# Batch 0's local q and k turned in halves, and batch 1's strided q and k loaded and turned earlier, in a fused sparse attention and MLP kernel

## The chip, the cores and the metric

The kernel runs on one core of a Trainium2 chip. The core has a tensor engine (PE, with its weight loads shown apart as PEld), a vector engine (DVE), a scalar engine (ACT), GpSimd (POOL) and a sync engine (SP) that only issues transfers. Each engine works through its own queue in order, and waits on semaphores where an instruction needs another engine's result or a transfer's landing. The metric is the device time of one execution in microseconds (us); lower is better.

## The reference

```python
# attention: batch 8, heads 8, sequence 576, head size 64; stride 32
scores = scale * np.matmul(q, k.transpose(0, 1, 3, 2))
rel = pos[:, None] - pos[None, :]
mask_local = (rel >= 0) & (rel < stride)                                     # heads 0 to 3
mask_strided = (rel >= 0) & (pos[None, :] % stride == pos[:, None] % stride) # heads 4 to 7
attn = softmax(np.where(masks, scores, -1e9)); attn_out = np.matmul(attn, v)
# MLP on x = attn_out as 4608 tokens of 512
h = x @ w_in                                  # 512 to 2048
g = np.maximum(h, 0.0) + alpha * np.minimum(h, 0.0)
out = g @ w_out                               # 2048 to 512
```

Both masks are sparse: a local query sees 32 keys at most, a strided one at most 18, so the kernel computes only blocks that can be nonzero.

## The kernel before

The 4608 tokens are nine chunks of 512. Each chunk goes through layer 1 (16 pieces of 128 hidden units, four matmuls each, `lin1_piece`) and layer 2. The attention of the eight batches is spread between these matmuls, so that TensorE always has some. Attention works on pairs of heads, four pairs a batch: pairs 0 and 1 are batch 0's local heads, 2 and 3 its strided heads, 4 and 5 batch 1's local heads, 6 and 7 its strided heads, and so on. This change touches only the opening, which is written out by hand: everything before layer 1 of chunk 0 (all of batch 0's attention), layer 1 of chunk 0, and a second list that mixes chunk 0's layer 2 with batch 1's attention. After that a planner spreads the pieces of later batches evenly.

The lists are made of short functions, and `keep` holds every engine to the order in which they are written:

- `F(nm, pr)` (`turn_first`) transposes batch 0's strided q or k on PE in float32. `G(nm, pr)` (`turn_second`, lines 160 to 169) does the same for batch 1 from the float16 tiles `qsd` and `ksd`, eight transposes and one copy: ACT copies q, DVE copies k. `pr` is 0 for the first strided pair of a batch, 1 for the second.
- `Cl(b, nm, eng)` (`cast_l`) casts local q or k (the tiles `ql` and `kl`) from float32 to float16 on POOL or ACT. `T(u, nm)` (`transpose_piece`, lines 254 to 273) then transposes it on PE, nine transposes into two PSUM banks of five and four, and copies the two banks out with ACT or DVE.
- `Sc(g, i)` (`score_piece`) computes half i of a pair's scores. Half 0 uses the double bank `sp` and one exponential on ACT; half 1 takes two single banks and two exponentials. `sc1(g)` (`score_both`) does both halves and masks them on DVE.
- `Pv(g, a)` (`pv_piece`) multiplies by V, then DVE takes the reciprocal of the sums (L413) and the product (L415).
- `X(g)` (`x_piece`) transposes a pair's output into the layer input `xT` and copies it out with ACT or DVE.
- `vs(b, pr)` casts strided V, `ov(b, eng, c0, c1)` (`over_v`) copies 32 rows of local V for the blocks c0 to c1, each from where the transfer put them to where the next block needs them.
- `L(m)` runs the first two of the four matmuls of layer 1's piece m; `lin1_piece(0, m)` later adds the other two. Each piece is followed by ACT (`neg`, L593) and DVE (`gT`, L596).
- `U(kf)` and `W(i)` are matmuls of chunk 0's layer 2. `w(1)` is one matmul on zeros, `alpha` a small transpose for the slopes.

PSUM has eight banks: three in the pool `ps`, three in `ph` (tag `hps`, used by layer 1 and by half 1 of the early scores), two in `sp`. The zero matmuls hold one `hps` bank until the last of them. Transfers that cast or that come late are issued from POOL's queue: V, W_in in four quarters, then batch 1's strided q and k (`load_d(1)`), its strided V, W_out in four quarters, batch 1's local q, k and V. POOL has eight transfers under way at most: the ninth waits for the first to land. SP's queue issues batch 0's q and k.

Of the kernel before, what the change touches and what calls it, by code (L numbers as in the profile page):

```python
# [10 lines left out]
F16 = mybir.dt.float16  # L11
# [21 lines left out]
def kernel(  # L33
# [10 lines left out]
    nc = tc.nc  # L44
    keep = tc.keep_in_program_order
# [11 lines left out]
    hpool = ctx.enter_context(tc.tile_pool(name="half", bufs=4))  # L57
# [5 lines left out]
    pspool = ctx.enter_context(tc.tile_pool(name="ps", bufs=3, space=bass.MemoryType.PSUM))  # L63
    phpool = ctx.enter_context(tc.tile_pool(name="ph", bufs=3, space=bass.MemoryType.PSUM))
# [9 lines left out]
    ident = consts[:, 0:128]  # L74
# [10 lines left out]
    qTs = [cpool.tile([128, 2, 672], F16, name=f"qT{i}") for i in range(2)]  # L85
    kTs = [cpool.tile([128, 2, 672], F16, name=f"kT{i}") for i in range(2)]
# [7 lines left out]
    loaded = {}  # L94
    cast16 = {}
# [32 lines left out]
                keep(nc.sync.dma_start_transpose(  # L128
                    o.rearrange("r (w p) -> r w p", p=96), t16[0:96, 768 * e : 768 * e + 768]))

    def load_d(b):

        for nm, src in (("q", q), ("k", k)):
            keep(nc.gpsimd.dma_start(
                qks[nm][0:72], src[b, 4:8, :, :].rearrange("h (p t) d -> p h (t d)", t=8)))

# [40 lines left out]
    def cast_l(b, nm, eng="pool"):  # L177
        t16 = hpool.tile([128, 9, 2, 64], F16, tag=f"{nm}l16", bufs=2, name=f"{nm}l16")
        cast_copy(eng, t16, loaded[(b, False, nm)].rearrange("p f (t d) -> p t f d", t=9))
        cast16[(b, False, nm)] = t16  # L180

    def load_v(b, strided):


        if strided:
            st = spool.tile([128, 2048], F16, tag="v", bufs=2, name="stv")
            step = 2 if b == 0 else 4
            for h in range(0, 4, step):
                keep(nc.gpsimd.dma_start(
                    st[0:72, 512 * h : 512 * (h + step)].rearrange("p (h e) -> p h e", h=step),  # L190
                    v[b, 4 + h : 4 + h + step, :, :].rearrange("h (p t) d -> p h (t d)", t=8)))
            loaded[b] = st
        else:
            v16 = vls[b % 2]
            base = v[b, 0:1, 0:1, :]
            r0 = 32 if b < 2 else 0
            step = 12 if b == 0 else 24
            for c in range(0, 24, step):
                keep(nc.gpsimd.dma_start(
                    v16[r0:128, c : c + step, 0:64],  # L200
                    bass.AP(tensor=base.tensor, offset=base.offset + (96 * c - 32 + r0) * D,
                            ap=[[D, 128 - r0], [96 * D, step], [1, D]])))
            cast16[(b, False, "v")] = v16

    def cast_copy(eng, o, i):
        if eng == "act":
            keep(nc.scalar.copy(o, i))
        elif eng == "dve":
            keep(nc.vector.tensor_copy(o, i))
        else:  # L210
            keep(nc.gpsimd.tensor_copy(o, i))  # L211

    def cast_v(b, pr, eng):

        v16 = vss[b % 2]
        cast_copy(eng, v16[0:72, 2 * pr : 2 * pr + 2, :, 0:64],
                  loaded[b][0:72, 1024 * pr : 1024 * pr + 1024].rearrange(
                      "p (h t d) -> p h t d", h=2, t=8))
        cast16[(b, True, "v")] = v16
# [12 lines left out]
    wide = {"on": True}  # L232
# [232 lines left out]
    def T(u, nm):  # L465
        return lambda: transpose_piece(u, nm)

    def Sc(g, i):
        return lambda: score_piece(pairs[g], i)

    def Pv(g, i):
        return lambda: pv_piece(pairs[g], i)

    def X(g, eng=None):
        return lambda: x_piece(pairs[g], eng or ("act" if pairs[g].strided else "dve"))

    for g in range(7, npair + 2):
        c = g // 4
        a, p, t = g, g - 1, g + 1
# [279 lines left out]
    def warm(n):  # L759

        for _ in range(n):
            keep(nc.tensor.matmul(wps, wrm[:, 0:128], wrm, start=True, stop=True))  # L762
# [11 lines left out]
            name=nc.get_next_instruction_name(), act_func_set_id=6, ins=[], outs=[]  # L774
# [35 lines left out]
    def F(nm, pr):  # L810
        return lambda: turn_first(nm, pr)
# [3 lines left out]
        keep(nc.tensor.transpose(apt[:, 0:16], alpha_r, id32[0:16, 0:16]))  # L815
        keep(nc.vector.tensor_scalar(oma, apt[:, 0:16], -1.0, 1.0, op0=ALU.mult, op1=ALU.add))

    def vs(b, pr):
        return lambda: cast_v(b, pr, "dve")

    def Cl(b, nm, eng="pool"):
        return lambda: cast_l(b, nm, eng)

    def ov(b, eng, c0, c1):
        return lambda: over_v(b, eng, c0, c1)

    def w(n):
        return lambda: warm(n)

    def L(m):  # L830
        return lambda: lin1_piece(0, m, True)

    def G(nm, pr):
        return lambda: turn_second(nm, pr, "act" if nm == "q" else "dve")

    warm(17)
    for fn in [
        F("q", 0), w(1), F("k", 0), w(1), F("k", 1), Sc(2, 0), vs(0, 0), w(1), F("q", 1), Sc(2, 1), alpha, Pv(2, 0),
        Sc(3, 1), vs(0, 1), Cl(0, "q"), Cl(0, "k"), Pv(2, 2), Sc(3, 0), w(1), Pv(3, 2), T(0, "q"), Pv(3, 0), w(1),
        Pv(3, 1), w(1), T(0, "k"), X(3), w(1), Sc(0, 1), Pv(2, 1), Sc(0, 0), Sc(1, 1), ov(0, "dve", 12, 24),  # L840
        ov(0, "pool", 0, 12), Pv(0, 1), X(2), Pv(0, 0), Sc(1, 0), Pv(1, 1), L(1), X(0, "act"), Pv(1, 0), L(2), L(3),
        X(1), L(0)]:
        fn()
    load_d(1)
    load_v(1, True)
    load_w(0, True)
    load_w(1, True)
# [2 lines left out]
    load_w(2, True)  # L850
    load_v(1, False)
    load_w(3, True)
    mid = {13: ("q", 0), 14: ("k", 0), 15: ("q", 1)}
    for m in range(16):
        lin1_piece(0, m)
        attn_n(0, 0)
# [14 lines left out]
    def U(kf):  # L871
        def run():
            if kf == 0:
                banks.extend(phpool.tile([128, 512], F32, tag="hps", name="ops") for _ in range(3))
            for mt in range(3):
                keep(nc.tensor.matmul(  # L876
                    banks[mt], gTs[0][:, kf, 128 * mt : 128 * mt + 128], wout16[:, kf, :],
                    start=(kf == 0), stop=(kf == 15)))
            if kf == 15:
                for mt in range(3):  # L880
                    osb = opool.tile([128, 512], F32, tag="osb", name="osb")
                    cast_copy("dve" if mt == 1 else "act", osb, banks[mt])
                    keep(nc.sync.dma_start(out[128 * mt : 128 * mt + 128, :], osb))
        return run
# [14 lines left out]
    def sc1(g):  # L899
        return lambda: score_both(pairs[g], "dve")  # L900

    for fn in [
        U(0), Cl(1, "q"), G("k", 1), vs(1, 0), vs(1, 1), sc1(6), U(1), U(2), sc1(7), Cl(1, "k", "act"), U(3), U(4), loads2,
        Pv(6, 0), Pv(7, 0), Pv(6, 2), U(5), Pv(7, 1), U(6), T(2, "q"), U(7), Pv(7, 2), T(2, "k"), Pv(6, 1), U(8),
        X(7, "dve"), W(0), W(1), sc1(4), U(9), W(2), sc1(5), W(3), ov(1, "dve", 0, 24), W(4), U(10), X(6), U(11),
        Pv(4, 1), W(5), Pv(4, 0), Cl(2, "q", "act"), U(12), Cl(2, "k", "act"), Pv(5, 1), U(13), U(14), Pv(5, 0), U(15), W(6), X(5), X(4), W(7)]:
        fn()
# [65 lines left out]
```

## Time and profile before

| what | value |
|---|---|
| median of 3 runs | 300.79 us (300.78 to 301.1) |
| profiled execution | 300.67 us, its span 298.9 us, granted clock 1.0 |
| PE busy in the span | 292.9 us (98%) |
| DVE, ACT, POOL busy | 219.1, 178.8, 172.8 us |
| matmuls of layer 1 (L585) | 576, 131.9 us of PE |
| first local scores of batch 0 | 17.41 us from the span's start |
| long run of layer 1 matmuls begins | 22.93 us |

The time of an execution is the span, in which instructions of the program run, and some 1.8 us around it. PE's busy time covers a matmul from its start to its modelled end, and matmuls overlap, so a PE that shows as busy may be waiting for a short while; the distance from one start to the next tells more. Below, a bracket at the end of a row gives the idle time of the engine ahead of it and what ended that.

### The profile page before, as it was taken

The numbers are of one execution on the slowest core, as the hardware profiler recorded it, in microseconds if no ns is written. First come the engines' busy times: TensorE is split into PE (matmuls) and PEld (weight loads), VectorE is DVE, ScalarE is ACT, GpSimd is POOL, SyncE is SP. The second block draws the span as 40 slices with busy tenths as digits, with TensorE's granted clock in tenths as the row PEclk, the third lists the DMA queues.
The fourth block names the chain that finished last, engine by engine and source line by source line (L and its number), as shares of the span: only waits on it lengthen the run. The fifth ranks groups of instructions, "written<-read, shape, count | busy, mean of one in ns | idle before, by whom it ended". The sixth has DMA issues, their size and how long they took to land.

```text
span 298.9 us, 6826 instructions
## 1 busy us (share of the span) xinstructions
PE 292.9 (98%) x2683; PEld 183.0 (61%) x2683; DVE 219.1 (73%) x408; ACT 178.8 (60%) x332; POOL 172.8 (58%) x160
## 2 busy tenths in 40 slices
PE   8999999999999999999999999999999999999995
PEld 3764555554545478646864687468745974784484
DVE  5677886668775897589848984898489958936852
ACT  1676755698457775776477646764676356516730
POOL 8362270049969998979897988495653405002300
PEclk9999999999999999999999999999999999999999
DMA  7999999999998969999989999955911040022004
GB/s 183 257 193 202 256 197 259 217 200 295 113 200 140 113 101 97 159 190 132 127 156 182 158 139 188 170 89 96 205 24 21 16 148 0 2 72 70 0 2 141
DMA packets 96977, 41.18 MB, mean 138 GB/s; under 512 B 75361, under 2 KB 93233, under 8 KB 96945
## 3 DMA queue, kind: packets, MB, share of 16 engines
q0 software_dynamic: 51008, 17.77, 60.7%
q1 hardware_dynamic: 45584, 22.32, 34.6%
q10 hardware_dynamic: 352, 0.66, 0.9%
q8 instruction: 21, 0.34, 0.5%
q14 instruction: 12, 0.09, 0.1%
HBM read 38.24 MB, written 9.44 MB: 160 GB/s over the span
## 4 chain that ended last, share of the span: by engine, by line
PE 82%; DVE 10%; ACT 3%; issue 3%; DVEq 0%; ACTq 0%
PE hps L585 37%; PE ops L720 18%; PE ops L624 5%; PE ops L710 4%; PE pv L406 4%; DVE gsum L654 2%; PE wps L762 2%; PE ops L876 2%; DVE gT L596 2%; DVE x L415 2%; PE sp L353 2%; DVE x16s L415 1%; ACT neg L593 1%; PE sph L353 1%; PE xp L431 1%
## 5 line engine op out<-in xcount | busy, mean ns | idle before, releaser
L585 PE MATMUL hps<-xT,win 128*128 128x512 f16 x576 | 131.9, 379 | 0.0
L596 DVE SCALAR_TENSOR_TENSOR gT<-neg,oma,hps 128x512 f16<-128x512 f32 x144 | 105.3, 744 | 36.1 <-ACT neg L593 28.1
L593 ACT ACTIVATE neg<-hps 128x512 f32<-128x512 f32 x144 | 85.8, 598 | 35.2 <-PE hps L585 33.0
L585 PEld LDWEIGHTS <-win 128*128 128x128 f16 x576 | 53.7, 98 | 58.9 <-issue 0.2
L654 POOL TENSOR_TENSOR gsum<-gT 128x1024 f16<-128x1024 f16 x14 | 29.7, 2123 | 41.7 <-DVE gT L596 36.7
L378 POOL TENSOR_TENSOR et<-et,consts 128x576 f16<-128x576 f16 (+1 forms) x24 | 35.5, 1481 | 30.2 <-ACT et L376 30.0
L720 PEld LDWEIGHTS <-gT 128*128 128x128 f16 x336 | 31.5, 98 | 5.4 <-issue 0.3
L415 DVE TENSOR_TENSOR x<-pv,rc 96x384 f16<-96x384 f32 (+2 forms) x62 | 33.0, 532 | 2.1
L385 POOL TENSOR_TENSOR et<-et,consts 128x576 f16<-128x576 f16 (+1 forms) x24 | 31.5, 1313 | 0.0
L406 PEld LDWEIGHTS <-et 72*128 72x128 f16 (+1 forms) x448 | 23.4, 98 | 11.5 <-issue 1.2
L720 PE MATMUL ops<-wout,gT 128*128 128x256 f16 x224 | 27.9, 272 | 0.1
L710 PE MATMUL ops<-wsum,gsum 128*128 128x256 f16 x216 | 26.6, 273 | 0.0
L376 ACT ACTIVATE et<-sp 128x576 f16<-128x576 f32 (+1 forms) x24 | 15.5, 645 | 17.1 <-PE sp L353 17.1
L720 PEld LDWEIGHTS <-gsum 128*128 128x128 f16 x224 | 20.9, 98 | 2.6
L710 PEld LDWEIGHTS <-gsum 128*128 128x128 f16 x224 | 20.8, 98 | 2.6
L413 DVE RECIPROCAL rc<-pv 96x6 f32<-96x6 f32 (+2 forms) x80 | 14.6, 183 | 10.6 <-PE pv L406 10.4
L211 POOL COPY vs<-stv 72x1024 f16<-72x1024 f16 x12 | 13.4, 1117 | 14.5 <-DMA stv<-in_v_dram 14.5
L665 DVE TENSOR_TENSOR osb<-ops,par 128x512 f32<-128x512 f32 (+1 forms) x14 | 9.4, 672 | 15.7 <-PE ops L720 8.2
L382 ACT ACTIVATE et<-sph 128x288 f16<-128x288 f32 (+1 forms) x48 | 18.8, 409 | 0.0
L663 ACT COPY osb<-ops 128x512 f32<-128x512 f32 x14 | 8.2, 587 | 16.7 <-PE ops L720 16.7
L624 PE MATMUL ops<-wout,gT 128*128 128x512 f16 x64 | 16.4, 379 | 0.0
L406 PE MATMUL pv<-vs,et 72*128 72x65 f16 x256 | 15.4, 193 | 0.7 <-DVE x L415 0.5
(107 smaller groups left out, 355.4 us busy)
## 6 DMA issues: line engine op xcount, KB each, us to landing
out_dram<-osb SPq DMA_DIRECT2D x35, 256.0 KB, 4.3
vl<-in_v_dram POOLq DMA_DIRECT2D x6, 384.0 KB, 9.0
win<-in_moe_w_in_dram POOLq DMA_DIRECT2D x4, 512.0 KB, 17.7
wout<-in_moe_w_out_dram POOLq DMA_DIRECT2D x4, 512.0 KB, 16.5
qsd<-in_q_dram POOLq DMA_DIRECT2D x7, 288.0 KB, 6.3
ksd<-in_k_dram POOLq DMA_DIRECT2D x7, 288.0 KB, 8.3
stv<-in_v_dram POOLq DMA_DIRECT2D x7, 288.0 KB, 8.0
ql<-in_q_dram SPq DMA_DIRECT2D x3, 576.0 KB, 6.9
```

Source lines behind the costliest of these rows:

```text
L378: keep(nc.gpsimd.tensor_tensor(mv, mv, m, op=ALU.mult))
L382: keep(nc.scalar.activation(ev[:, n * y : n * y + n], sps[y][0:r, 0:n], AF.Exp, scale=SCALE))
L385: keep(nc.gpsimd.tensor_tensor(mv, mv, m, op=ALU.mult))
L406: keep(nc.tensor.matmul(pv[:, 65 * x : 65 * x + 65], et[0:r, c : c + 128], v16[0:r, 2 * P.pr + hh, t, :] if P.strided else v16[:, 6 * (2 * ...
L415: keep(nc.vector.tensor_tensor(P.x16[0:w, c0 : c0 + 64 * nb].rearrange("r (c e) -> r c e", e=64), pvv[:, :, 0:64], rc[0:w, 0:nb].unsqueeze ...
L585: keep(nc.tensor.matmul(hps, win16[:, kk, 128 * m : 128 * m + 128], xT[:, kk, c0 : c0 + 512], start=(kk == 2), stop=(kk == 1)))
L593: keep(nc.scalar.activation(neg, hps, AF.Relu, scale=-1.0))
L596: keep(nc.vector.scalar_tensor_tensor(gTs[n][:, m, :], neg, oma[:, m : m + 1], hps, op0=ALU.mult, op1=ALU.add))
L624: keep(nc.tensor.matmul(ops, gTs[n][:, kf, 128 * mt : 128 * mt + 128], wout16[:, kf, :], start=(kf == 0), stop=(kf == 15)))
L654: keep((nc.vector if eng == "dve" else nc.gpsimd).tensor_tensor(gsum[i][:, hs], a, b, op=op))
L710: keep(nc.tensor.matmul(o, gsum[i][:, y, 128 * z : 128 * z + 128], wsum[i][:, y, :], start=(x == "5" and y == 0 and (z == 0 or alone)), st ...
L720: keep(nc.tensor.matmul(o, lhs(y), rhs(y), start=(first and y == 0), stop=(y == 7), skip_group_check=True))
```

## The change

- `load_d` takes the names of the tensors to load, and batch 1's two strided loads are issued inside the opening list instead of behind it: `ld("q")` after the casts of q and k, `ld("k")` between the two copies of V rows. Both copies are now on POOL (`ov(0, "pool", 0, 12)` and `ov(0, "pool", 12, 24)`); the second was on DVE.
- Batch 0's local q and k are cast and turned in halves (five and four of the nine positions) by `cast_h` and `turn_h`. POOL casts both halves of q and the second of k, ACT the first of k. Two of the four halves go through banks of the pool `hps` instead of `ps`. DVE copies out the second half of k, ACT the other three.
- Batch 1's strided q and k are turned after pieces 12, 13, 14 and 15 of layer 1, in the order q 0, k 0, k 1, q 1. Before, q 0, k 0 and q 1 came after pieces 13, 14 and 15, and k 1 after the first of layer 2's matmuls.
- Batch 1's strided V is cast by POOL at the head of the second list instead of by DVE.
- The opening list has a new order: `alpha` before pair 2's second half, pair 3's half 0 before its half 1, pair 2's output before the local scores and on DVE, local scores from half 0 on, the half pieces of layer 1 in the order 0, 3, 2, 1, and one `w(1)` more. In the second list `U(0)` comes after the scores of pair 6 and `U(2)` after those of pair 7.

```diff
--- before.py
+++ after.py
@@ -128,9 +128,10 @@
                 keep(nc.sync.dma_start_transpose(
                     o.rearrange("r (w p) -> r w p", p=96), t16[0:96, 768 * e : 768 * e + 768]))
 
-    def load_d(b):
-
-        for nm, src in (("q", q), ("k", k)):
+    def load_d(b, nms="qk"):
+
+        for nm in nms:
+            src = q if nm == "q" else k
             keep(nc.gpsimd.dma_start(
                 qks[nm][0:72], src[b, 4:8, :, :].rearrange("h (p t) d -> p h (t d)", t=8)))
 
@@ -178,6 +179,28 @@
         t16 = hpool.tile([128, 9, 2, 64], F16, tag=f"{nm}l16", bufs=2, name=f"{nm}l16")
         cast_copy(eng, t16, loaded[(b, False, nm)].rearrange("p f (t d) -> p t f d", t=9))
         cast16[(b, False, nm)] = t16
+
+    def cast_h(nm, h, eng):
+
+        if (0, False, nm) not in cast16:
+            cast16[(0, False, nm)] = hpool.tile(
+                [128, 9, 2, 64], F16, tag=f"{nm}l16", bufs=2, name=f"{nm}l16")
+        t0, t1 = ((0, 5), (5, 9))[h]
+        cast_copy(eng, cast16[(0, False, nm)][:, t0:t1], loaded[(0, False, nm)].rearrange(
+            "p f (t d) -> p t f d", t=9)[:, t0:t1])
+
+    def turn_h(nm, h, eng, wide):
+
+        t0, t1 = ((0, 5), (5, 9))[h]
+        dst = qTs[0][:, :, 0:576] if nm == "q" else kTs[0][:, :, 32:608]
+        pool, tag = (phpool, "hps") if wide else (pspool, "ps")
+        tp = pool.tile([128, 8, 64, 2], F16, tag=tag, name="tp")
+        for t in range(t0, t1):
+            keep(nc.tensor.transpose(
+                tp[:, t - t0].rearrange("r p e -> r (p e)"),
+                cast16[(0, False, nm)][:, t].rearrange("p f d -> p (f d)"), ident))
+        cast_copy(eng, dst.rearrange("r e (p t) -> r e p t", t=9)[:, :, :, t0:t1],
+                  tp[:, 0 : t1 - t0].rearrange("r t p e -> r e p t"))
 
     def load_v(b, strided):
 
@@ -815,8 +838,8 @@
         keep(nc.tensor.transpose(apt[:, 0:16], alpha_r, id32[0:16, 0:16]))
         keep(nc.vector.tensor_scalar(oma, apt[:, 0:16], -1.0, 1.0, op0=ALU.mult, op1=ALU.add))
 
-    def vs(b, pr):
-        return lambda: cast_v(b, pr, "dve")
+    def vs(b, pr, eng="dve"):
+        return lambda: cast_v(b, pr, eng)
 
     def Cl(b, nm, eng="pool"):
         return lambda: cast_l(b, nm, eng)
@@ -833,15 +856,24 @@
     def G(nm, pr):
         return lambda: turn_second(nm, pr, "act" if nm == "q" else "dve")
 
+    def Ch(eng, nm, h):
+        return lambda: cast_h(nm, h, eng)
+
+    def ld(nms):
+        return lambda: load_d(1, nms)
+
+    def Th(nm, h, eng, wide=False):
+        return lambda: turn_h(nm, h, eng, wide)
+
     warm(17)
     for fn in [
-        F("q", 0), w(1), F("k", 0), w(1), F("k", 1), Sc(2, 0), vs(0, 0), w(1), F("q", 1), Sc(2, 1), alpha, Pv(2, 0),
-        Sc(3, 1), vs(0, 1), Cl(0, "q"), Cl(0, "k"), Pv(2, 2), Sc(3, 0), w(1), Pv(3, 2), T(0, "q"), Pv(3, 0), w(1),
-        Pv(3, 1), w(1), T(0, "k"), X(3), w(1), Sc(0, 1), Pv(2, 1), Sc(0, 0), Sc(1, 1), ov(0, "dve", 12, 24),
-        ov(0, "pool", 0, 12), Pv(0, 1), X(2), Pv(0, 0), Sc(1, 0), Pv(1, 1), L(1), X(0, "act"), Pv(1, 0), L(2), L(3),
-        X(1), L(0)]:
+        F("q", 0), w(1), F("k", 0), w(1), F("k", 1), Sc(2, 0), vs(0, 0), w(1), F("q", 1), alpha, Sc(2, 1), Pv(2, 0),
+        Sc(3, 0), w(1), Sc(3, 1), vs(0, 1), Ch("pool", "q", 0), Ch("pool", "q", 1), Ch("pool", "k", 1), ld("q"), Pv(2, 2), w(1),
+        Th("q", 0, "act"), Pv(3, 2), w(1), Pv(2, 1), w(1), Ch("act", "k", 0), Th("q", 1, "act", True), Th("k", 1, "dve"),
+        Th("k", 0, "act", True), w(1), Pv(3, 1), Pv(3, 0), X(2, "dve"), Sc(0, 0), Sc(0, 1), ov(0, "pool", 0, 12),
+        ld("k"), ov(0, "pool", 12, 24), X(3), Pv(0, 0), Sc(1, 0), Pv(0, 1), Sc(1, 1), Pv(1, 0), L(0), Pv(1, 1), L(3), X(0, "act"), L(2),
+        X(1), L(1)]:
         fn()
-    load_d(1)
     load_v(1, True)
     load_w(0, True)
     load_w(1, True)
@@ -850,7 +882,7 @@
     load_w(2, True)
     load_v(1, False)
     load_w(3, True)
-    mid = {13: ("q", 0), 14: ("k", 0), 15: ("q", 1)}
+    mid = {12: ("q", 0), 13: ("k", 0), 14: ("k", 1), 15: ("q", 1)}
     for m in range(16):
         lin1_piece(0, m)
         attn_n(0, 0)
@@ -900,7 +932,7 @@
         return lambda: score_both(pairs[g], "dve")
 
     for fn in [
-        U(0), Cl(1, "q"), G("k", 1), vs(1, 0), vs(1, 1), sc1(6), U(1), U(2), sc1(7), Cl(1, "k", "act"), U(3), U(4), loads2,
+        vs(1, 0, "pool"), vs(1, 1, "pool"), Cl(1, "q"), sc1(6), U(0), U(1), sc1(7), Cl(1, "k", "act"), U(2), U(3), U(4), loads2,
         Pv(6, 0), Pv(7, 0), Pv(6, 2), U(5), Pv(7, 1), U(6), T(2, "q"), U(7), Pv(7, 2), T(2, "k"), Pv(6, 1), U(8),
         X(7, "dve"), W(0), W(1), sc1(4), U(9), W(2), sc1(5), W(3), ov(1, "dve", 0, 24), W(4), U(10), X(6), U(11),
         Pv(4, 1), W(5), Pv(4, 0), Cl(2, "q", "act"), U(12), Cl(2, "k", "act"), Pv(5, 1), U(13), U(14), Pv(5, 0), U(15), W(6), X(5), X(4), W(7)]:
```

## The prediction

> **What bounds the kernel now.** I read the page's busy shares first, then the timeline of each engine from 10 to 42 us, where the change lies, and the tiles' landings. From the page:
>
> ```profile
> PE 292.9 (98%) x2683; PEld 183.0 (61%) x2683; DVE 219.1 (73%) x408; ACT 178.8 (60%) x332; POOL 172.8 (58%) x160
> ```
>
> TensorE is the bound: what is gained or lost in its queue early comes out at the end, unless something that does not move (a landing) stops it later. "Busy" hides short waits, so I read PE's rows by their starts (start us, busy us, engine, line, operation, count):
>
> ```profile
> 13.72 0.82 PE L269 MATMUL tp<-consts,ql 128*128 128x128 f16 x9
> 14.78 0.34 PE L406 MATMUL pv<-vs,et 72*128 72x65 f16 x6 [0.24 <-DVE x L415]
> 15.61 0.78 PE L269 MATMUL tp<-consts,kl 128*128 128x128 f16 x9
> 16.68 0.43 PE L431 MATMUL xp<-consts,x 72*128 72x72 f16 x8 [0.29 <-DVE x L415]
> 17.41 0.30 PE L295 MATMUL sph<-qT,kT 64*128 64x96 f16 x6
> ...
> 22.93 11.02 PE L585 MATMUL hps<-xT,win 128*128 128x512 f16 x50
> ...
> 36.29 0.82 PE L876 MATMUL ops<-wout,gT 128*128 128x512 f16 x3
> ...
> 37.44 0.80 PE L353 MATMUL sph<-qT,kT 64*128 64x72 f16 x8
> 38.17 1.47 PE L876 MATMUL ops<-wout,gT 128*128 128x512 f16 x6
> ```
>
> Nine transposes take 0.50 when nothing stops them (59.75 to 60.25), yet q's and k's take 1.06 and 1.07 from start to next start: about 1.1 us of waits. The first local scores start at 17.41, after k's copy. The solid stretch of layer 1 begins at 22.93; the two first multiplications close piece 0's half, so the 48 others start at 23.36. The eight score matmuls at 37.44 take 0.73 to 38.17, where the same eight at 39.71 take 0.23: a wait of 0.5. The other engines' rows that decide:
>
> ```profile
> 12.70 0.70 ACT L316 ACTIVATE et<-sph 72x288 f16<-72x288 f32 x2 [0.60 <-PE sph L311]
> 13.53 0.65 ACT L319 ACTIVATE et<-sp 72x576 f16<-72x576 f32 x1
> 14.20 1.36 ACT L207 COPY qT<-tp 128x640 f16<-128x640 f16 x2
> 16.09 0.77 ACT L207 COPY kT<-tp 128x640 f16<-128x640 f16 x1 [0.53 <-PE tp L269]
> ...
> 36.23 0.60 ACT L593 ACTIVATE neg<-hps 128x512 f32<-128x512 f32 x1 [0.53 <-PE hps L585]
> 36.73 0.63 ACT L207 COPY qT<-tf 128x576 f16<-128x576 f16 x1
> 41.05 1.15 ACT L207 CAST kl<-kl 128x1152 f16<-128x1152 f32 x1
> ```
>
> ```profile
> 10.22 0.43 DVE L209 COPY vs<-stv 72x1024 f16<-72x1024 f16 x1
> 12.66 0.88 DVE L209 COPY vs<-stv 72x1024 f16<-72x1024 f16 x1
> 16.55 0.71 DVE L209 COPY kT<-tp 128x512 f16<-128x512 f16 x1
> ```
>
> ```profile
> 12.12 1.14 POOL L211 CAST ql<-ql 128x1152 f16<-128x1152 f32 x1 [3.92 <-DMA ql<-in_q_dram]
> 14.03 1.15 POOL L211 CAST kl<-kl 128x1152 f16<-128x1152 f32 x1 [0.77 <-DMA kl<-in_k_dram]
> 16.06 0.78 POOL L211 COPY vl<-vl 32x715 f16<-32x715 f16 x1 [0.88 <-DMA vl<-in_v_dram]
> 39.22 1.25 POOL L211 CAST ql<-ql 128x1152 f16<-128x1152 f32 x1 [6.86 <-DMA ql<-in_q_dram]
> ```
>
> **Prices, from PE's start to the next start.** A score half 0.49 (0.58 before another); PV of six 0.18 (0.29 before scores), of four 0.12; a warm matmul 0.22 to 0.25; an output transpose 0.27; a half piece of layer 1 0.43 to 0.46; one strided turn 0.26. An ACT exponential starts 0.69 after a score half in the double bank, 0.57 in single banks, and holds ACT 0.55, or 0.30 for each single one. The reciprocal starts 0.39 after its PV, the product ends 0.76 later. A hand-over to PE costs 0.06.
>
> **Step 1, order to the first transposes.** Nothing moves up to 10.22. Pair 3's single-bank half waited on PE for pair 2's exponentials; now its double-bank half goes first. On PE: alpha 10.72, scores 10.90, PV 11.39, scores 11.68, warm 12.17, scores 12.39, PV 12.88, warm 13.00, q's first five transposes 13.25 (13.72 before). ACT ends pair 3's exponentials at 13.67 instead of 14.18. The change adds one warm matmul, 0.22, which is in this count.
>
> **Step 2, turns in halves.** q's first copy follows its transposes by 0.48 (13.72 to 14.20): 13.73, ACT free at 14.40. Then ACT casts 5/9 of k, landed at 3.46 + 10.5 = 13.96: 5/9 of 1.15 is 0.64, taken as 0.68, to 15.08; the upper bound is the whole cast's 1.15. Behind it ACT holds q's second copy (to 15.63) and k's (from PE's transposes at 15.14: 15.62 to 16.39); a late cast moves both. DVE's half of k is done by 16.14. POOL's casts (some 0.7 and 0.6 for q, 0.6 for k from 14.03) are needed only at 14.50 and 14.74, and the layer-1 banks are free by then, so these cost nothing, up to 0.2 more included. First local scores: 16.47 instead of 17.41, a gain of 0.94.
>
> **Step 3, to the solid stretch.** PE's starts: scores of pair 0 at 16.47 and 17.05, X(3) 17.57, PV 17.87, scores of pair 1 18.16, PV 18.65, scores 18.94, then PV of pair 1 waits for an ACT exponential that stands behind X(3)'s copy, 19.57 (a wait of 0.14); L(0) 19.82, PV 20.28, L(3) 20.48, X(0) 20.94, L(2) 21.21, X(1) 21.67, L(1) 21.94, the rest 22.40. That is 5.93 after the first scores, 5.95 before: PV and X have traded places, the wait at 22.27 is gone, two small ones came. Gain at the stretch: 0.96. L(0) needs W_in's first quarter, landed at 4.75 + 15.0 = 19.75: no slack, where the half piece at 20.70 had 0.95.
>
> **Step 4, POOL's queue.** q's strided load now goes out at some 14.6 (16.79), ahead of the V copy that waits for its rows until 16.06; k's at 16.84 (17.54), behind that copy and ahead of the second, which has gone from DVE (0.36 at 19.09) to POOL: from 17.57, some 0.85, done 18.4, needed at 19.57. Both loads landed at 30.1 and 31.0, the turns come at some 32.0 and 33.1. The next issues keep their times: each waits for the landing eight loads before (20.01, 22.56, 25.09, 28.36 in POOL's rows). Batch 1's two strided V casts go to POOL after their landing at 33.0 and end by 35.2, before PV at 40.7; DVE's 0.75 there (37.90) saved nothing that PE waited for. Price 0; if V rows came over 1.1 us later, PV of pair 1 would wait.
>
> **Step 5, the turn of strided q and k.** Three turns now precede piece 15's end, two before: 36.03 - 0.96 + 0.26 = 35.33. Then the last q turn to 35.59 and scores of pair 6 at 35.69. Their single-bank half needs that turn copied out by ACT, behind piece 15's "neg": 35.53, the copy 36.03 to 36.66, PE goes on at 36.74 and is through at 36.99. U(0), 0.65, which lay ahead of the scores, comes after: 37.64 against 38.17. The wait is 0.93 where 0.5 was; 0.43 of the gain is given back. Bounds: 0.5 (nothing given back) and 1.3 (neg 0.4 late behind DVE). From there the same work, 3.08 us, leads to pair 6's PV: 40.72 instead of 41.25. DVE's chain of products starts with it, so it too moves by 0.53, and no landing is in the way (W_out's third quarter 43.6 against 45.3).
>
> **A lock between DVE and POOL.** The V cast at 12.66 took 0.88 beside POOL's cast, 0.43 at 10.22. POOL's cast at 39.22 is tied to a landing (39.06) and stays, while pair 7's masks (40.60 and 41.20 before) come to 39.4 and 40.0, into it. By the 12.66 row, where DVE got on 0.15 before POOL's end, both are done at 41.1, just when the first product is due: price 0, upper bound 0.1 if DVE gets on only at POOL's end.
> The Trainium skill, SBUF — State Buffer, "Who interferes with whom", speaks against this overlap: an operation of DVE with two SBUF inputs is shut out for the whole of a GpSimd operation that reads SBUF. By that rule the masks end at 41.24 and the sum would be 0.42 instead of 0.53, 300.25, inside the forecast's own range and its chance; the trace agrees with the blocking itself (0.88 against 0.43).
>
> **Sum.** -0.94 - 0.02 + 0.43 = -0.53. The profiled execution took 300.67 (span 298.9 and 1.8 around it): 300.14. The median of the runs is 0.12 above it, so 300.2 on either account. What one can tell from no change is 0.2%, 0.6 us, so the forecast stands at its edge.
>
> **Rivals.** *The full early gain stays*: PE's wait at pair 6's scores is no longer than the old 0.5. For it: DVE has fewer casts there. Against: the row at 36.73 puts q's copy behind neg on ACT. It gives 300.67 - 0.96 = 299.7. *The split brings nothing*: ACT's cast of part of k costs the 1.15 of a whole one, or its wait shifts the exponentials behind it; 0.47 lost, 300.6. Against: ACT's time follows the size (0.65 for 576 elements, 0.77 for 640, 1.15 for 1152). *Slower*: the strided q load, queued 2.2 us sooner, shares the engines with W_in's quarters instead of following them. For it: they land 2.5 to 3.3 us apart, so the queue is full, and L(0) has no slack. Half of q's load (some 1.2 us, as between the landings of q, k and V) would put L(0) 1.2 us later, and all behind it: 300.14 + 1.2, 301.4. It decides once the quarter lands 0.5 us late. Against: every landing follows the order of issue.
>
> **How the numbers follow.** Forecast 0.50, rivals 0.18, 0.17 and 0.15. The likeliest case has 299.8 to 300.6 as its own range; 299.5 to 301.0 takes in the first two rivals and leaves out the third and a few hundredths. Faster by over 0.2% means under 300.19: the first rival and half of the forecast, 0.43; within: the other half and nearly all of the second rival, 0.41; slower 0.16.
>
> **What would show it.** Right: first local scores near 16.5; ACT's cast of 640 elements near 0.7; the stretch of layer 1 at 22.4; a wait of 0.9 inside pair 6's scores, ended by ACT; a mask near 39.4 of 1.2 us. Wrong: L(0) waiting for a W_in landing, W_in's quarters later than 19.75, 22.5, 25.1 and 28.3, or PV of pair 1 waiting for POOL.

## The result, and the profile after

The changed kernel takes 300.11 us (median of 14 runs, 299.75 to 300.49) beside 300.62 (14 runs of the kernel before on the same chip): ratio 0.9982, 95% interval 0.9974 to 0.9990. That is 0.5 us less, just inside the 0.2% that I called no change. On a second chip the same kernel took 300.20 beside 300.77, ratio 0.9980 (0.9971 to 0.9989). The profiled execution took 300.08, its span 298.3.

The page's first row after the change: TensorE is the bound as before, with one instruction more (the warm matmul).

```profile
PE 292.3 (98%) x2684; PEld 182.7 (61%) x2684; DVE 219.1 (73%) x406; ACT 178.5 (60%) x332; POOL 175.5 (59%) x164
```

TensorE's rows of the timeline after (start us, busy us, engine, line, operation, count, and in brackets the idle time before it and what ended it):

```profile
13.34 0.45 PE L199 MATMUL tp<-consts,ql 128*128 128x128 f16 x5
...
14.37 0.39 PE L199 MATMUL tp<-consts,ql 128*128 128x128 f16 x4
...
15.25 0.45 PE L199 MATMUL tp<-consts,kl 128*128 128x128 f16 x5 [0.23 <-ACT kl L230]
...
16.54 0.30 PE L318 MATMUL sp<-qT,kT 64*128 64x96 f16 x6
...
19.99 0.61 PE L608 MATMUL hps<-xT,win 128*128 128x512 f16 x2
...
22.00 10.15 PE L608 MATMUL hps<-xT,win 128*128 128x512 f16 x46
...
35.73 0.30 PE L376 MATMUL sp<-qT,kT 64*128 64x72 f16 x8
36.24 0.19 PE L376 MATMUL sph<-qT,kT 64*128 64x72 f16 x1 [0.21 <-DVE kT L232]
36.75 0.29 PE L376 MATMUL sph<-qT,kT 64*128 64x72 f16 x7 [0.32 <-ACT qT L230]
36.97 1.47 PE L908 MATMUL ops<-wout,gT 128*128 128x512 f16 x6
...
40.69 0.65 PE L429 MATMUL pv<-vs,et 72*128 72x65 f16 x16
```

The first local scores start at 16.54 (17.41 before). The two first multiplications in the row at 22.00 close piece 0's half, so the solid stretch begins at 22.43 (23.36 before). U(0) starts at 36.97 behind both halves of pair 6's scores, and pair 6's PV at 40.69 (41.25 before). The rows of the other engines that answer to those shown of before:

```profile
13.83 0.76 ACT L230 COPY qT<-tp 128x640 f16<-128x640 f16 x1 [0.29 <-PE tp L199]
14.47 0.72 ACT L230 CAST kl<-kl 128x640 f16<-128x640 f32 x1
...
35.57 0.60 ACT L616 ACTIVATE neg<-hps 128x512 f32<-128x512 f32 x1 [0.53 <-PE hps L608]
36.06 0.63 ACT L230 COPY qT<-tf 128x576 f16<-128x576 f16 x1
...
12.28 0.43 DVE L232 COPY vs<-stv 72x1024 f16<-72x1024 f16 x1
...
39.39 1.77 DVE L396 TENSOR_TENSOR et<-et,consts 72x576 f16<-72x576 f16 x2 [1.08 <-ACT et L390]
41.09 0.18 DVE L436 RECIPROCAL rc<-pv 72x6 f32<-72x6 f32 x1
...
12.31 1.53 POOL L234 CAST ql<-ql 128x640 f16<-128x640 f32 x2 [4.08 <-DMA ql<-in_q_dram]
...
39.41 1.44 POOL L234 CAST ql<-ql 128x1152 f16<-128x1152 f32 x1 [4.15 <-DMA ql<-in_q_dram]
```

One profile against one other misleads here by more than half a microsecond, because executions of one kernel begin their opening at different times (the changed kernel's first transpose at 7.11 in one profile and at 7.77 in another). So I cut each profiled span at three landmarks: the first transpose of the opening (F(q,0)), the solid stretch, and the end of the last multiplication. The table has the time of the first and then the lengths of the three stretches behind it, called opening, middle and last stretch below. The runs of the next section stand in the same table; "n" is the number of runs behind a median, and `again` is a second run of the changed kernel as it is.

| kernel | us (n) | ratio to before | first transpose at | to the solid stretch | to TensorE's end | to the span's end |
|---|---|---|---|---|---|---|
| before | 300.62 (14) | 1 | 7.46 | 15.90 | 272.31 | 3.18 |
| after | 300.11 (14) | 0.9982 (0.9974–0.9990) | 7.11 | 15.32 | 272.63 | 3.19 |
| again | 300.20 (10) | 0.9980 (0.9971–0.9989) | 7.77 | 14.95 | 272.63 | 3.21 |
| open_alone | 300.61 (11) | 0.9998 (0.9989–1.0007) | 7.11 | 15.01 | 272.68 | 3.95 |
| second_alone | 301.97 (5) | 1.0033 (1.0021–1.0046) | 7.42 | 16.14 | 272.60 | 3.99 |
| u0_first | 299.42 (5) | 0.9952 (0.9940–0.9965) | 7.12 | 15.00 | 272.26 | 3.17 |
| vcast_later | 300.65 (11) | 0.9996 (0.9987–1.0005) | 7.41 | 15.91 | 272.61 | 3.20 |
| pad2 | 301.10 (11) | 1.0015 (1.0006–1.0023) | 7.46 | 15.01 | 272.64 | 4.04 |
| open_vpool | 302.54 (8) | 1.0070 (1.0044–1.0096) | 6.89 | 15.37 | 277.94 | 3.18 |
| u0_vdve | 300.67 (11) | 0.9995 (0.9984–1.0005) | 7.12 | 15.00 | 272.70 | 3.99 |
| open_vfirst | 300.39 (12) | 0.9990 (0.9980–1.0000) | 7.24 | 15.00 | 273.73 | 3.17 |
| whole | 300.82 (11) | 1.0002 (0.9994–1.0011) | 7.84 | 15.93 | 272.67 | 3.19 |
| ld_late | 300.24 (11) | 0.9983 (0.9973–0.9992) | 7.25 | 15.14 | 272.62 | 3.18 |
| u0_between | 299.62 (7) | 0.9970 (0.9956–0.9984) | 7.15 | 15.30 | 272.10 | 3.18 |

The kernel before took 300.86, 300.77, 300.73 and 300.68 beside the four groups of runs. Between before and after the opening gets shorter, some of that is given back in the middle, and the last stretch stays: the shape of the forecast. The runs were to tell whether its reasons hold.

### The profile page after: what moved, and what is told of

Same layout as the page of the kernel before. It is cut to its first block, busy times and chain, and to the rows that moved or that the text cites. A ratio compares the mean times of both kernels' runs of the same rounds, so it can differ in the third digit from the quotient of the medians.

```text
span 298.3 us, 6835 instructions
## 1 busy us (share of the span) xinstructions
PE 292.3 (98%) x2684; PEld 182.7 (61%) x2684; DVE 219.1 (73%) x406; ACT 178.5 (60%) x332; POOL 175.5 (59%) x164
## 4 chain that ended last, share of the span: by engine, by line
PE 80%; DVE 8%; ACT 4%; DMA 3%; issue 3%; SPq 1%; POOL 0%; DVEq 0%; ACTq 0%
PE hps L608 38%; PE ops L743 18%; PE ops L647 5%; PE ops L733 5%; PE pv L429 4%; DMA ql<-in_q_dram 3%; DVE gsum L677 2%; PE ops L908 2%; PE sp L376 2%; DVE gT L619 2%; DVE x16s L438 1%; ACT neg L616 1%; PE sph L376 1%; PE xp L454 1%; DVE x L438 1%
## 5 line engine op out<-in xcount | busy, mean ns | idle before, releaser
L234 POOL COPY vs<-stv 72x1024 f16<-72x1024 f16 x14 | 15.3, 1104 | 16.5 <-DMA stv<-in_v_dram 16.5
L760 ACT COPY par<-ops 128x512 f32<-128x512 f32 x13 | 7.6, 585 | 14.0 <-PE ops L733 14.0
```

## Experiments

All kernels compute the whole reference.

**The opening alone, the second list alone.** The first (open_alone) undoes the second half of the change:

```diff
-    mid = {12: ("q", 0), 13: ("k", 0), 14: ("k", 1), 15: ("q", 1)}
+    mid = {13: ("q", 0), 14: ("k", 0), 15: ("q", 1)}
-        vs(1, 0, "pool"), vs(1, 1, "pool"), Cl(1, "q"), sc1(6), U(0), U(1), ...
+        U(0), Cl(1, "q"), G("k", 1), vs(1, 0), vs(1, 1), sc1(6), U(1), U(2), ...
```

> The changed opening alone, with the old places of the strided turns (after pieces 13, 14, 15, and k 1 behind U(0)), the old second list and its V casts on DVE. Theory (the opening wins 0.9 us at TensorE and the later turn gives 0.4 back): faster than the full change, about 299.7 us, 0.9 below the kernel before; in its trace pair 6's PV starts near 40.3 instead of 40.7, and the score matmuls of pair 6 wait 0.5, not 0.9. Rival (the early win is cut by a landing whatever comes later, here W_out's first quarter at 35.2 or the casts tied to landings near 39.4 and 40.7): same as the full change, 300.1, with PV of pair 6 at 40.7.

The second (second_alone) keeps before's opening and takes the new mid and second list.

> The old opening with only the earlier strided turns, the new head of the second list and its V casts on POOL; the strided loads stay behind the opening. Theory: slower than the kernel before by the 0.43 us that the longer wait at pair 6's scores costs, about 301.05. Rival (the second part gains by itself, since DVE loses two casts): 300.4 or lower.

Both missed by 0.9 us (300.61 and 301.97), both on the slow side. The table shows that most of it lies where neither theory looked: behind the last multiplication, 3.95 and 3.99 where before and after have 3.2. Up to there the second list alone ended 0.49 later than before. Only 0.29 came in the middle, where 0.43 was expected; 0.24 came in its opening, which is that of the kernel before, and so a spread between executions (and it began 0.04 earlier). The opening alone ended 0.87 earlier, 0.35 of which is the earlier first transpose. In its middle it lost 0.37 all the same. Rows of the opening alone, VectorE, POOL and TensorE:

```profile
39.36 1.55 DVE L396 TENSOR_TENSOR et<-et,consts 72x576 f16<-72x576 f16 x2 [1.13 <-ACT et L390]
...
39.09 1.14 POOL L234 CAST ql<-ql 128x1152 f16<-128x1152 f32 x1 [6.85 <-DMA ql<-in_q_dram]
...
40.60 0.48 PE L429 MATMUL pv<-vs,et 72*128 72x65 f16 x10 [0.24 <-DVE et L396]
```

The two masks took 1.55 beside POOL's cast (0.91 for the pair at 37.32, with no cast beside it) and TensorE waited 0.41 at pair 7's PV for the first of them, which took 1.19 and was done at 40.55. This is the lock between VectorE and POOL that I had priced at 0 for the changed kernel: where such instructions of the two overlap, one holds up the other. There the PV of pairs 6 and 7 come 0.7 later, and the price is 0.

**U(0) ahead of pair 6's scores (u0_first).**

```diff
-        vs(1, 0, "pool"), vs(1, 1, "pool"), Cl(1, "q"), sc1(6), U(0), U(1), ...
+        vs(1, 0, "pool"), vs(1, 1, "pool"), Cl(1, "q"), U(0), sc1(6), U(1), ...
```

> The full change, but U(0) ahead of pair 6's scores again, where its 0.65 us lies in the wait for q's copy. Theory: the wait inside pair 6's scores falls from 0.9 to 0.3, U(1) starts near 37.0 instead of 37.6, PV of pair 6 near 40.05, the time 299.5, 0.6 below the full change. Rival (U(0) only moves the wait to W_out's landing or to the casts near 39.4 and 40.7): 300.1, with PV of pair 6 at 40.7 or a new wait ahead of it.

Measured 299.42, ratio 0.9952 (0.9940 to 0.9965): as the theory said, and faster than both kernels. TensorE around the wait:

```profile
35.35 0.81 PE L908 MATMUL ops<-wout,gT 128*128 128x512 f16 x3
36.09 0.30 PE L376 MATMUL sp<-qT,kT 64*128 64x72 f16 x8
36.23 0.49 PE L376 MATMUL sph<-qT,kT 64*128 64x72 f16 x8
36.65 0.82 PE L908 MATMUL ops<-wout,gT 128*128 128x512 f16 x3
```

Both halves of pair 6's scores take 0.56 from start to next start (36.09 to 36.65) where the changed kernel took 1.24 (35.73 to 36.97). The middle took 272.26, what it took before the change. So what was given back is TensorE's wait inside pair 6's scores, and it is not forced.

**The V cast behind POOL's casts (vcast_later).** `vs(0, 1)` moved behind `Pv(2, 2)` in the opening list, so that VectorE leaves the port to POOL's q casts.

> The full change, but DVE's cast of pair 3's V stands behind the product of pair 2's third PV, out of the way of GpSimd's first cast of q. In the trace of the changed kernel that cast and the next took 1.53 together beside DVE's 0.43, and the chain runs from q's landing (12.25) through it. Theory (the lock costs 0.3 on the chain): q's first transposes start 0.25 sooner after q's landing, the first local scores too, time 299.85. Rival (ACT's exponentials hold the copy anyway, or TensorE then waits for the later V cast): no change, 300.1.

300.65: slower than theory and rival said, by what the rival named, a wait for the later V cast. TensorE, VectorE and POOL in the opening:

```profile
14.81 0.28 PE L429 MATMUL pv<-vs,et 72*128 72x65 f16 x4 [1.03 <-DVE vs L232]
...
13.88 0.79 DVE L232 COPY vs<-stv 72x1024 f16<-72x1024 f16 x1
...
13.77 0.61 POOL L234 CAST kl<-kl 128x512 f16<-128x512 f32 x1 [0.58 <-DMA kl<-in_k_dram]
```

The later cast met POOL's k cast instead of its q casts, took 0.79, and TensorE waited 1.03 for it at a PV. The opening is back at 15.91: the place of one cast of 0.43 can undo the whole gain there. The theory failed too. POOL's first q cast fell to 0.72, yet q's transposes started at 13.34, 1.48 behind q's landing (1.09 in the profile of after): here they followed the instructions ahead of them in TensorE's queue, and not the cast.

**The stretch behind the last multiplication (pad2, again, open_vpool, open_vfirst, u0_vdve).** The four runs so far with 3.2 us there, and the two with 4.0, had the same stores and the same last multiplications. What differed in order was the length of VectorE's instruction stream (waits included): 455 instructions before, 452 in the changed kernel, u0_first and vcast_later; 454 and 453 in the two with 4.0. (The traces themselves show two fewer in every kernel; the differences are the same.) An 8 KB packet of an instruction queue falls among the last stores' packets in every trace: 1.6 us after TensorE's end in the two with 4.0, about 1.9 to 2.2 in those with 452, and before TensorE's end in the kernel before. The eight later traces agree: 1.6 in the two with 4.0, 1.9 to 2.2 in the six with 452. A theory, then: this packet is a fetch of instructions, the length of the stream moves it, and where it meets the last stores the end comes later. To try it, two small memsets more at VectorE's beginning, of columns that are set to zero there anyway, and nothing else (the stream then has 453 instructions).

```diff
+    keep(nc.vector.memset(kTs[0][:, :, 0:32], 0.0))
+    keep(nc.vector.memset(kTs[0][:, :, 0:32], 0.0))
```

> The changed kernel with two more small memsets among VectorE's first (of columns that are set to zero there anyway), long before anything waits for VectorE. VectorE's instruction stream is then as long as in the kernel with the new second list alone (453 against 452), and every wait, transfer and multiplication is that of the changed kernel. Theory (the stretch behind the last multiplication depends on where VectorE's instruction fetch falls among the last stores' packets): TensorE's end stays at 295.1, the stretch behind it grows from 3.2 to 4.0, 300.9. Rival (the 0.8 us in the runs with the opening alone and the second list alone came from their own order of work): stretch 3.2, 300.1.

> The changed kernel, unaltered, on the chip of the three other runs of this group. Both theories: 300.1, TensorE's end 295.1 us into the span, 3.2 us from there to the span's end.

301.10 against 300.20 on the same chip. TensorE's part is that of the unaltered kernel to 0.07 (15.01 and 272.64), the last stretch 4.04 against 3.21. The transfers from 293.5 on in the changed kernel (bytes moved in 40 equal slices of that stretch, then the last two stores: tile, queue, count, size, us from issue to landing):

```profile
GB/s 391 391 378 391 145 0 0 0 0 0 0 0 0 50 353 397 391 347 259 384 233 57 0 0 0 0 0 0 0 0 0 0 0 0 0 0 0 0 0 0
...
out_dram<-osb SPq DMA_DIRECT2D x1, 256.0 KB, 2.2
out_dram<-osb SPq DMA_DIRECT2D x1, 128.0 KB, 1.7
```

and the same of pad2:

```profile
GB/s 378 391 378 391 215 6 0 0 0 0 0 0 0 6 309 384 397 378 227 422 271 25 13 13 6 19 0 0 0 0 0 0 0 0 0 0 0 0 0 0
...
out_dram<-osb SPq DMA_DIRECT2D x1, 256.0 KB, 2.2
out_dram<-osb SPq DMA_DIRECT2D x1, 128.0 KB, 2.6
```

The last store trickles out over five slices (6 to 25 GB/s), four of them behind the changed kernel's last, and lands 0.9 later. Two memsets 290 us earlier did that. That the fetch itself holds up some of the store's packets is argued from where it falls; moving the fetch alone was not tried, and the trace does not tell which engine's instructions the packet holds.

Two more runs use the theory. One gives the opening alone a stream of 452, by V casts on POOL:

```diff
-        U(0), Cl(1, "q"), G("k", 1), vs(1, 0), vs(1, 1), sc1(6), ...
+        U(0), Cl(1, "q"), G("k", 1), vs(1, 0, "pool"), vs(1, 1, "pool"), sc1(6), ...
```

> The changed opening and order with the second list of before, as in the run with the opening alone, but batch 1's two V casts (both on VectorE there) on POOL, so that VectorE's stream has 452 instructions instead of 454. Theory (fetch among the last stores): TensorE's end as in that run, 294.8, the stretch behind it 3.2 instead of 4.0, 299.75, which is what my sum gives for the full early gain. Rival (VectorE's stream does not matter): 300.6 as in that run.

The last stretch came out as expected, 3.18, but the time was 302.54. I had put the V casts behind POOL's q cast. First POOL and TensorE, then stretches of 2 us (length; busy us and count of PE, its weight loads, DVE, ACT and POOL; granted clock; time share of the DMA engines; GB/s):

```profile
39.81 1.14 POOL L234 CAST ql<-ql 128x1152 f16<-128x1152 f32 x1 [7.07 <-DMA ql<-in_q_dram]
40.90 2.47 POOL L234 COPY vs<-stv 72x1024 f16<-72x1024 f16 x2
...
42.21 0.34 PE L429 MATMUL pv<-vs,et 72*128 72x65 f16 x6 [1.47 <-POOL vs L234]
43.42 0.71 PE L429 MATMUL pv<-vs,et 72*128 72x65 f16 x10 [0.87 <-DVE x L438]
43.94 1.47 PE L908 MATMUL ops<-wout,gT 128*128 128x512 f16 x3
```

```profile
42.00:44.00 2.00, 0.92 (x17) 0.82 (x17) 1.26 (x4) 0.96 (x1) 2.00 (x3) 0.72 3.52 102
44.00:46.00 2.00, 2.00 (x14) 0.90 (x12) 1.40 (x5) 0.00 (x0) 2.00 (x3) 0.50 2.03 153
```

The cast waits for a landing at 39.69, the V casts stand behind it in POOL's queue, and TensorE waits 1.47 and 0.87 for them and what follows. The granted clock falls to 0.50 at 42.87, 0.3 into the second wait (0.72 is the mean from 42 to 44), and stays there until 49.69: three multiplications take 1.47 where three take 0.81 elsewhere. So 5.3 us were lost in this execution; in five of the eight the clock stayed at 1.0 and the time was 301.5 to 302.7.

The order mended, both V casts at the head of the second list:

> As the run with the opening alone and the V casts on POOL (302.5), but with both casts at the head of the second list, ahead of the q cast on POOL, which waits for a landing near 39. Theory: the 1.6 us of wait in that run were V casts queued behind that q cast, and its lower clock came from this wait; they are gone. VectorE's stream has 452 instructions, so the stretch behind TensorE's last multiplication is 3.2. What stays is the wait of 0.4 at pair 7's PV for a mask on VectorE that runs beside POOL's q cast: TensorE's end 294.8 as with the opening alone, 299.8. First rival (the stream does not matter): 300.6. Second rival (the two V casts on POOL cost more than their place in its queue): over 301 again.

300.39 (299.58 to 301.11), between the theory's 299.8 and the first rival's 300.6. By the time alone the first rival is the nearer. But the last stretch is 3.17, not the 4.0 of the opening alone, so the stream theory holds a third time, and the second rival is out. What the theory missed lies in the middle. TensorE in the profiled execution, which took 300.96:

```profile
36.14 0.82 PE L908 MATMUL ops<-wout,gT 128*128 128x512 f16 x3 [0.80 <-DMA wout<-in_moe_w_out_dram]
...
41.74 0.48 PE L429 MATMUL pv<-vs,et 72*128 72x65 f16 x10 [0.40 <-DVE et L396]
```

With U(0) first in the list, TensorE comes to W_out's first quarter as it lands: 36.09 here, 34.94 in the run with the opening alone. The wait for the mask is there too.

The other run puts the V casts of u0_first back on VectorE, which makes its stream 454:

> The changed kernel with U(0) ahead of pair 6's scores, and batch 1's two V casts back on VectorE, behind U(0) (VectorE's stream: 454). Theory (V casts cost nothing on TensorE's path, but the longer stream moves the fetch into the last stores): TensorE's end 294.4 as in the run with U(0) ahead and the V casts on POOL, the stretch behind it 4.0, 300.2. First rival (the stream does not matter): 299.4. Second rival (VectorE's casts delay the masks of pairs 6 and 7, TensorE ends later): over 294.7, with a wait for VectorE at pair 6's or 7's PV.

300.67. The last stretch is 3.99 as the theory had it. TensorE's end was 294.82, not 294.4; but what it waited for was not VectorE:

```profile
45.00 0.81 PE L908 MATMUL ops<-wout,gT 128*128 128x512 f16 x3 [0.54 <-DMA wout<-in_moe_w_out_dram]
```

W_out's third quarter landed at 44.96 here and at 44.33 in u0_first, where the same row starts at 44.57. So the gain of u0_first ends where W_out's quarters begin, and how much of it is left varies from run to run.

**Halves against whole casts (whole).** Batch 0's local q and k cast and turned as before the change, in the changed order:

```diff
-        ... Ch("pool", "q", 0), Ch("pool", "q", 1), Ch("pool", "k", 1), ld("q"), Pv(2, 2), w(1),
-        Th("q", 0, "act"), Pv(3, 2), w(1), Pv(2, 1), w(1), Ch("act", "k", 0), Th("q", 1, "act", True), Th("k", 1, "dve"),
-        Th("k", 0, "act", True), w(1), Pv(3, 1), ...
+        ... Cl(0, "q"), Cl(0, "k"), ld("q"), Pv(2, 2), w(1),
+        T(0, "q"), Pv(3, 2), w(1), Pv(2, 1), w(1), T(0, "k"), w(1), Pv(3, 1), ...
```

> The changed kernel, but batch 0's local q and k cast whole on POOL and transposed nine at a time through the double bank, as before; order of pairs 3 and 2, strided loads and second list as in the changed kernel. Theory (order is worth 0.47, halves are worth 0.47): first local scores near 17.1 instead of 16.5, stretch of layer 1 near 23.0, 300.6. First rival (the halves bring nothing, the order brings all): 16.5, 300.1. Second rival (the order alone brings nothing, since q's landing sets the start of its transposes): 17.4 and 300.8.

300.82, ratio 1.0002 against the changed kernel's 0.9980: the halves are worth 0.6 us, uncertain by 0.4. The first rival is out. The time alone does not tell my theory from the second rival, and TensorE's rows of the profiled execution (301.49, the longest of the eleven) do not either:

```profile
16.11 0.68 PE L292 MATMUL tp<-consts,kl 128*128 128x128 f16 x9 [0.44 <-POOL kl L234]
...
17.95 0.30 PE L318 MATMUL sp<-qT,kT 64*128 64x96 f16 x6
```

k landed at 14.85 in it (13.47 to 14.31 in the thirteen other traces), and its cast held up the transposes. The order shows in the distance from the first transpose to q's transposes: 6.25 and 6.50 in the two kernels with the old order, 5.92 to 6.05 in eleven with the new, this one (5.98) among them, and 6.22 only in the profile of after. The order is worth some 0.3 to 0.5. Part of that is the lock: in the old order the first PV of pair 3 stands ahead of q's transposes and needs the V cast that POOL's cast holds up. In the profile of before that cast was done at 13.54 and the PV started at 13.60, 0.05 later than TensorE's queue allowed; in second_alone it was 0.16.

**The place of the strided loads in POOL's queue (ld_late).** `load_d(1)` behind the opening list again.

> The changed kernel with batch 1's strided q and k loads issued behind the whole opening list on POOL, as a test of the place in its queue. Theory (price 0: the loads land a little later, still ahead of the turns near 32 and 33): 300.1, same start of the layer-1 stretch, no wait for a landing at the turns. First rival (the loads issued early hold up W_in's first quarter or the V rows): L(0) up to 0.3 earlier, 299.8. Second rival (late loads miss the turns): a wait at 32 to 34 for the landing, 301 or more.

300.24: the theory. POOL and TensorE:

```profile
17.71 0.75 POOL L135 DMA_DIRECT2D qsd<-in_q_dram  x1
18.45 0.72 POOL L135 DMA_DIRECT2D ksd<-in_k_dram  x1
...
19.95 0.60 PE L608 MATMUL hps<-xT,win 128*128 128x512 f16 x2
```

q's load went out at 17.71 instead of 14.51 and landed at 30.36 instead of 30.26; k's at 31.46 instead of 31.20. W_in's first quarter landed at 19.90 instead of 19.95, which says little, as it landed between 19.20 and 19.96 in the fourteen traces; the time says more. Neither rival is left.

**U(0) inside pair 6's scores (u0_between).** If the given-back time is one wait, it can be filled where it stands:

```diff
+            if i and between is not None:
+                between()
...
-        ... Cl(1, "q"), sc1(6), U(0), U(1), sc1(7), ...
+        ... Cl(1, "q"), sc1(6, U(0)), U(1), sc1(7), ...
```

> The changed kernel with U(0) issued between the two halves of pair 6's scores, so that its three multiplications stand where TensorE waits for ScalarE's copy of q. The copy's time does not change (36.06 to 36.7), so the second half still starts near 36.8, but U(0)'s 0.65 is then done. Against U(0) ahead of both halves, U(0) starts near 36.1 instead of 35.35 and so leaves 0.8 to W_out's first quarter, which landed at 34.9 to 36.1 in the runs so far. Theory (what was given back is that one wait, and it can be filled): U(1) near 37.0, TensorE's end 0.5 to 0.65 earlier than in the changed kernel, 299.5. First rival (the copy of q moves too, for want of a bank or because neg comes later): 300.1. Second rival (W_out's third quarter, landed at 43.7 to 45.0, becomes the next wait in front of the U that needs it): 299.8 to 300.1 with a wait for a landing near 44.5.

299.62, ratio 0.9970 (0.9956 to 0.9984), TensorE:

```profile
35.73 0.30 PE L378 MATMUL sp<-qT,kT 64*128 64x72 f16 x8
35.97 0.82 PE L910 MATMUL ops<-wout,gT 128*128 128x512 f16 x3
36.72 0.32 PE L378 MATMUL sph<-qT,kT 64*128 64x72 f16 x8
36.98 0.82 PE L910 MATMUL ops<-wout,gT 128*128 128x512 f16 x3
```

The first half starts at 35.73 and U(1) at 36.98, where U(0) stood in the changed kernel. The three multiplications are gone from the path, the wait with them, and U(0) has 0.9 of slack behind W_out's first quarter (35.06). Its middle, 272.10, is the shortest of all. Both kernels beat the one before. By the intervals u0_first also beats the changed kernel, while u0_between can't be told apart from either by its time.

## Why the prediction was right

The forecast was 300.2 (its sum 300.14), the profiled execution took 300.08, the medians 300.11 and 300.20. 0.18% and 0.20% less than before is the edge between "same" and "faster", where the forecast had put it.

**Step 1 (order).** Forecast 13.25 for q's first transposes, measured 13.34. That the two are so near is luck. "Nothing moves up to 10.22" did not hold: in the profile of after all began 0.35 earlier, and lost it again. q landed at 12.25 whatever TensorE did, and VectorE's V cast started at 12.28, 0.03 ahead of POOL's first q cast, which took 0.97 instead of the 0.72 of ten other runs. I had the lock the wrong way round: I took the V cast to be held behind POOL, as it was in nine of those ten (where it took 0.45 to 0.97). From the start of before, 7.46, the usual distance of 5.98 gives 13.44, so against that profile the order is worth 0.28 and not 0.47.

**Step 2 (halves).** From q's first transposes to the first local scores 3.20 (forecast 3.22, before 3.69). ScalarE's cast of 640 elements took 0.72 (forecast 0.68, bound 1.15), and one part of k's transposes waited 0.23 for it. From q's first transposes to the solid stretch it was 9.09 here and 9.02 in `again`, forecast 9.15, before 9.64: this part gained a little more than forecast, where the order gained less. The rival that the split brings nothing is out by the run with whole casts.

**Step 3 (to the solid stretch).** 5.89 from the first scores, forecast 5.93, and the stretch at 22.43, forecast 22.40. The whole opening was 15.90 before; in the nine traces with all of the new opening it was 14.95 to 15.01 in six and 15.30 to 15.37 in three, so the forecast gain of 0.96 is what most of them show. The profile of after is one of the three (0.58) and comes to the same time by its earlier start. L(0) starts at 19.99, 0.04 behind the landing of W_in's first quarter: no slack, as said. In u0_first, where that quarter landed at 19.20, L(0) started at 19.63.

**Step 4 (POOL's queue).** Price 0, shown by the run with late loads to about 0.4 us. The slower rival, that the early load shares engines with W_in, is out by it.

**Step 5 (turn of q and k).** The step that carried the forecast. Forecast and measured: neg 35.53 and 35.57, the copy 36.03 and 36.06, the second half goes on at 36.74 and 36.75, U(0) 36.99 and 36.97, pair 6's PV 40.72 and 40.69. Given back by that PV: 0.43 forecast, 0.93 - 0.56 = 0.37 measured; by the end of TensorE's work 0.32. Two runs that fill the wait get it back, which also shows that the rival "the full early gain stays" failed for the reason given.

**The lock at pair 7's masks.** Forecast 41.1 for the first product, measured 41.09. But of the two masks only the second was held: the first started at 39.39, 0.02 ahead of POOL's cast, and took its usual 0.46 while the cast took 1.44 (1.14 in most other runs). The second mask started at 39.99, took 1.17 and ended at 41.16, 0.31 behind POOL's cast. Pair 7's first PV started at 40.87, before that, so it waits for the first mask alone. In `again` POOL's cast came first, and the first mask was done only at 40.61; the PV came at 41.16, and the price was 0 there too. In the opening-alone kernel, and in open_vfirst, the PV was due before the first mask was done, and waited 0.41 and 0.57. So my 0 to 0.1 was right for this order only, and no property of the overlap.
The Trainium skill, SBUF — State Buffer, "Who interferes with whom", has it that whichever of the two starts first keeps the shared port for its whole instruction. The trace agrees in both directions (the mask held here, POOL's q cast held in the opening), except that the mask's 0.45 must have begun some 0.14 before the recorded end of POOL's cast.

**What the sum lacked.** It went to TensorE's end and took what follows as fixed. That held here (3.18 and 3.19) by luck, the accident of 452 instructions; with 453, as in pad2, the same work measured 301.10, slower than before.

## What to carry to other kernels

Follow an early gain to the next engine whose queue holds what the bound engine needs; here it was one copy behind one activation, and three ready multiplications put into the wait took 0.5 us more off TensorE's path. Look then at the landings: once the wait was filled, W_out's quarters, which move with no engine, could become the limit (TensorE waited 0.54 for one in u0_vdve, and for none in u0_between). And when two variants differ by less than 1 us, cut the span at landmarks and look at the last stores first, because an edit can change them without touching any work.

## What the runs showed of the hardware that I had not expected

- Behind the last multiplication a span can end 0.8 us later with the same work. It came with the length of one engine's instruction stream: 3.17 to 3.21 in nine traces with 452 instructions on VectorE, 3.95 to 4.04 in four with 453 or 454, 3.18 in the one with 455. With 453 the last store's packets trickle (pad2 and second_alone: landed 2.6 and 2.5 after issue instead of 1.7). With 454 (the opening alone and u0_vdve) VectorE's last sum also started 0.45 after TensorE's end instead of 0.10, and the last store landed 2.1 to 2.2 after issue. The Trainium skill, Runtime: NRT & Kernel Launch, "Instruction fetch mechanics", calls the cost of such a fetch mostly hidden; here it does not seem to be, where it meets the last stores.
- Two waits of TensorE of 1.47 and 0.87 us, 0.3 us of work between them, came with a granted clock of 0.50 for 6.8 us. The Trainium skill, TensorE: Matmul & The Clock Gate, "Part 1: The HAM clock gate", names an idle window of about 3.4 us for that; here the clock fell 0.3 into the second wait, after 1.8 us of idle time in all, with TensorE busy for 1.7 of the 3.5 us ahead. The mean clock fell in three of eight executions of this kernel.
- A load issued 3.2 us later landed 0.1 later, as if the bytes queued ahead of it, and not its issue, set its landing (argued from this one pair of traces). W_out's first quarter landed anywhere between 34.9 and 36.2 over the runs, which sets how early layer 2 can begin.
